# Two tables of a planned decode kernel replaced: the moves of its four engine lists, and the constant products in TensorE's list

## The chip, the cores and the metric

The kernel runs on one core of one Trainium2 chip. The metric is the device time of one execution in microseconds. A measurement of it is the median over several executions; the profile is of one execution more, with a time of its own. The core has TensorE (PE, matmuls), VectorE (DVE), ScalarE (ACT), GpSimd (POOL), SyncE (SP, which issues the loads) and 16 DMA engines that move data from the chip's memory into the core's own memory.

## The reference

One new token for each of four sequences goes through two identical layers: attention over a cache of 4096 keys and values, then a gated feed-forward block, each behind a layer norm without weights and with its input added. Both layers use the same caches and the same weights; everything is bf16.

```python
def attention(x, k_cache, v_cache, wq, wo):      # x: 4 x 1 x 512
    q = heads(x @ wq)                            # 32 query heads of 128, 4 to a K/V head
    k = repeat(k_cache, 4); v = repeat(v_cache, 4)   # caches: 4 x 8 x 4096 x 128
    p = softmax(q @ k.T * 128 ** -0.5)
    return concat_heads(p @ v) @ wo              # wo: 4096 x 512

def feed_forward(x, w_gate, w_up, w_down):       # 512 x 1792, 512 x 1792, 1792 x 512
    return (sigmoid(x @ w_gate) * (x @ w_up)) @ w_down

x = x + attention(layernorm(x), ...)
x = x + feed_forward(layernorm(x), ...)
x = x + attention(layernorm(x), ...)             # the same caches and weights again
x = x + feed_forward(layernorm(x), ...)
```

The bytes are in the caches: 4 x 8 heads x 4096 x 128 x 2 bytes is 33.6 MB for K and as much for V, and the second layer needs them a second time, apart from what the kernel keeps.

## The kernel before

The work is cut into 16 units: one batch row, one half of the K/V heads (four of eight) and one layer each. A string, UNITS, gives their order, in which the rows run staggered: row 0 has finished its first layer while row 2 has not begun. K and V come in pieces of 0.5 MB (half a head, 2048 keys) into a ring of 27 slots, some as a whole head of 1 MB in two slots, and a list names those that are kept for the second layer. All 155 loads are issued by SyncE into one queue, in a written order, and a load waits until the last reader of its slot is done.

A unit runs so. VectorE transposes a K slot in place (line 853). TensorE multiplies it with the row's queries into S_ps (L864), four 512-column matmuls side by side on strips of the array. VectorE takes the maximum (L887), ScalarE the exponentials (L901), TensorE turns them through PT_ps (L912), and with the V slots they give O_ps (L999). Then the output projection wo (L1022, L1044, or L943 and L958 by rows) adds to the row's x.

After the last unit of a row in the first layer comes that row's **chain**, a string of small dependent steps on one row: layer norm (TensorE L1127, L1131 and VectorE L1135), gate and up products (L1201), the sigmoid through a tanh on ScalarE and the product on VectorE (L1244), the down product (L1258), the new x and the sums for the next layer norm (L1104 is the matmul that adds them up), and the queries of the second layer (L759 to L830). The rows' chains stand at about 81 to 98, 123 to 140 and 188 to 205 us for rows 0 to 2 and 232 to 250 us for row 3. A last chain, for all rows that end in the second layer, stands at 270 to 282 us, behind the last load.

The order is not the program's. Every operation is first recorded with its engine, cost, rank and dependences; then `schedule` places all of them in time by a model of the engines and the loads, assigns ring slots, and leaves one list per engine. Then `rearrange` edits these lists by two tables:

- MOVES: each word is one move. `p28>22` takes the operation at place 28 of TensorE's list and inserts it at place 22. The letters are s (SyncE's loads), a (ScalarE), p (TensorE) and d (VectorE), and the words act one after the other.
- FILLS: each word is one **constant product**, a matmul of a constant 128 x 128 matrix with constant columns into a bank that nobody reads before it is written anew (line 1446). `87.2.d64.a17` puts one of 2 x 256 columns ahead of place 87 of TensorE's list (as it is after the moves), and makes it wait for operation 64 of VectorE's list and 17 of ScalarE's. A first wait letter a chooses the bank PT_ps, d the bank G_ps. The result is used for nothing; such a product keeps TensorE at work.

`emit` then writes each engine's list, with a semaphore wait for each dependence that is not yet met on that engine. Ring slots and the tiles of all other operations are chosen before `rearrange` and do not depend on the tables.

Of the kernel before, what the change touches and what calls it, by code (L numbers as in the profile page):

```python
# [32 lines left out]
MOVES = "s21>0 s2>1 s8>2 s4>3 s14>4 s19>5 s13>6 s9>7 s9>8 s18>9 s15>10 s15>11 s19>12 s20>13 s21>14 s21>15 s21>16 s21>17 s20>18 s23>20 s23>21 s24>23 s27>25 s29>27 s30>28 s31>29 s34>33 s40>39 s45>44 s53>52 s58>57 s62>61 s71>70 s78>75 s78>76 s84>83 s87>86 s91>89 s91>90 s94>93 s102>101 s103>102 s118>115 s119>118 s120>119 s123>122 s124>123 s127>126 s136>134 s147>145 s147>146 s150>148 s150>149 s151>150 a2>1 a3>2 a7>6 a12>11 a24>23 a25>24 a31>30 a34>33 a35>34 a42>40 a42>41 a43>42 a44>43 a45>44 a46>45 a59>58 a61>60 a66>65 a67>66 a68>67 a70>68 a74>73 a75>74 a76>75 a77>76 a78>77 a79>78 a80>79 a81>80 a82>81 a83>82 a84>83 a85>84 a87>85 a87>86 a88>87 a89>88 a90>89 a92>90 a92>91 a94>92 a94>93 a96>94 a96>95 a97>96 a98>97 a99>98 a100>99 a101>100 a115>114 a120>119 a121>120 a125>124 a126>125 a127>126 a128>127 a142>141 p3>2 p28>22 p29>24 p28>25 p30>29 p40>39 p41>40 p45>41 p43>42 p44>43 p45>44 p46>45 p50>46 p48>47 p51>48 p50>49 p61>60 p62>61 p63>62 p71>65 p72>67 p93>90 p94>91 p97>92 p131>130 p132>131 p133>132 p134>133 p156>154 p157>156 p158>157 p159>158 p160>159 p161>160 p162>161 p163>162 p165>164 p166>165 p167>166 p168>167 p169>168 p171>169 p172>170 p173>171 p174>172 p175>173 p175>174 p184>183 p215>213 p222>217 p223>218 p224>219 p223>221 p230>226 p236>235 p237>236 p238>237 p239>238 p240>239 p241>240 p244>242 p250>249 p251>250 p252>251 p274>273 p275>274 p276>275 p283>282 p284>283 p285>284 p286>285 p287>286 p288>287 p292>291 p293>292 p294>293 p295>294 p300>297 p302>301 p303>302 p304>303 p305>304 p306>305 p307>306 p308>307 p310>308 p311>309 p312>310 p313>311 p313>312 p314>313 p315>314 p321>320 p322>321 p323>322 p344>342 p344>343 p345>344 p351>349 p352>350 p353>351 p373>371 p377>374 p405>403 p408>407 p410>409 p411>410 p412>411 p413>412 p414>413 p422>420 p423>422 p424>423 p425>424 p431>430 p432>431 p433>432 p434>433 p435>434 p436>435 p437>436 p441>437 p439>438 p440>439 p441>440 p443>442 p448>443 p445>444 p446>445 p447>446 p448>447 p459>455 p463>462 p464>463 p465>464 p466>465 p474>473 p481>479 p482>480 p503>499 p507>503 p508>504 p506>505 p507>506 p509>507 p509>508 p510>509 p533>532 p537>533 p541>538 p542>541 p560>559 p562>560 p593>592 p594>593 p602>600 p604>603 p605>604 p607>606 p633>631 d2>0 d14>1 d18>2 d16>3 d18>4 d18>6 d23>8 d21>10 d21>11 d27>12 d23>13 d15>14 d28>15 d28>17 d28>18 d29>20 d23>21 d27>22 d28>23 d32>24 d26>25 d27>26 d31>27 d41>32 d34>33 d35>34 d36>35 d37>36 d41>39 d43>42 d44>43 d46>44 d47>45 d48>47 d49>48 d51>50 d53>51 d53>52 d57>56 d60>59 d86>80 d82>81 d91>88 d90>89 d93>92 d95>93 d96>95 d97>96 d98>97 d99>98 d101>99 d102>101 d103>102 d105>103 d105>104 d107>105 d107>106 d108>107 d109>108 d120>119 d121>120 d126>124 d126>125 d128>127 d134>133 d136>134 d137>136 d141>139 d142>140 d143>141 d143>142 d144>143 d146>144 d148>145 d149>146 d149>147 d151>148 d152>149 d154>150 d154>151 d155>153 d158>154 d157>155 d159>157 d162>158 d161>159 d163>160 d166>162 d164>163 d165>164 d169>165 d170>166 d172>167 d172>170 d172>171 d174>172 d174>173 d175>174 d177>175 d178>176 d180>178 d180>179 d181>180 d182>181 d183>182 d184>183 d185>184 d186>185 d187>186 d188>187 d192>191 d193>192 d196>194 d202>201 d206>205 d207>206 d208>207 d209>208 d210>209 d211>210 d212>211 d213>212 d215>214 d217>216 d218>217 d219>218 d221>219 d222>220 d225>224 d230>226 d229>228 d232>231 d239>233 d241>235 d237>236 d239>238 d240>239 d247>246 d253>252 d254>253 d262>261 d265>264 d282>281 d283>282 d284>283 d285>284 d286>285 d287>286 d292>291 d295>293 d313>312 d314>313 d315>314 d316>315 d317>316 d318>317 d320>319 d322>321 d324>323 d328>327 d330>329"  # L33
# [55 lines left out]
class _Plan:  # L89
# [61 lines left out]
    def schedule(self):  # L151
# [205 lines left out]
        self.prog = {e: sorted((o for o in self.ops if o.eng == e), key=lambda o: (o.start, o.n)) for e in ENGINES}  # L357
        if FILLS:
            self.rearrange(fillers)
# [10 lines left out]
    def rearrange(self, fillers):  # L370
# [3 lines left out]
        queue["p"][:] = [op for op in queue["p"] if id(op) not in gone]  # L374
        for word in MOVES.split():
            i, j = map(int, word[1:].split(">"))
            queue[word[0]].insert(j, queue[word[0]].pop(i))
        ahead = {}
        for word in FILLS.split():
            at, n, *waits = word.split(".")  # L380
# [1108 lines left out]
```

## Time and profile before

| | |
|---|---|
| three runs | 287.33, 285.98, 284.43 us (median 285.98) |
| the profiled execution | 283.75 us, its span from first to last instruction 281.9 us |
| mean granted TensorE clock in the span | 0.958 |
| busy: TensorE, VectorE, ScalarE | 205.7, 159.0, 67.2 us |
| loaded | 106.70 MB, 378 GB/s over the span |
| constant products | 226, of them 111 of 256 columns |

How to read it: times are of one execution. The page cuts the span into 40 slices; a digit of an engine's row is the busy share in tenths, of the row PEclk the TensorE clock that was granted. A row of a table of stretches gives the stretch, its length, busy time and count for PE, PEld (weight loads), DVE, ACT and POOL, the granted clock, the DMA share and GB/s. A timeline row gives start, duration, engine, line, operation, what is written from what, how many instructions, and in brackets the idle time before and what ended it. A matmul's row includes the time in which it runs through the array, so that rows overlap.

### The profile page before, as it was taken

How to read it: one execution, taken by the hardware profiler on the slowest of the kernel's cores; microseconds unless marked ns; L12 is line 12 of the kernel's file. 1: busy time of each engine (PE TensorE's matmuls, PEld its weight loads, DVE VectorE, ACT ScalarE, POOL GpSimd, SP SyncE). 2: the span in 40 equal slices, each digit the busy share in tenths (PEclk: the TensorE clock that was granted, in tenths of full speed). 3: DMA queues.
4: the chain of work that ended last, by engine and by line, in shares of the span. 5: the costliest groups of instructions: out<-in, count | busy, mean ns of one | idle time of the engine just before them, and what ended most of it. 6: DMA issues, size and time to landing. Idle time of an engine off the chain costs nothing.

```text
span 281.9 us, 7386 instructions
## 1 busy us (share of the span) xinstructions
PE 205.7 (73%) x3212; PEld 102.0 (36%) x3212; DVE 159.0 (56%) x347; ACT 67.2 (24%) x169; POOL 15.7 (6%) x61
## 2 busy tenths in 40 slices
PE   0000068729779899998998768889886889899975
PEld 0000022303246542465533212346532346555453
DVE  1479924143502278713398799438469827976333
ACT  1000021200422231342311400431324142235411
POOL 8300010000000000000000000000000000000011
PEclk9999999957995899999999979999999999999999
DMA  7999999999999799999999999999999999999920
GB/s 282 420 422 414 410 388 389 381 428 412 401 402 408 262 353 421 418 414 404 398 392 413 417 420 424 427 406 411 409 408 406 417 416 400 352 381 391 409 80 3
DMA packets 27536, 107.18 MB, mean 380 GB/s; under 512 B 2544, under 2 KB 6640, under 8 KB 23408
## 3 DMA queue, kind: packets, MB, share of 16 engines
q1 hardware_dynamic: 27440, 106.70, 95.4%
q8 instruction: 25, 0.41, 0.6%
q14 instruction: 7, 0.06, 0.1%
q10 hardware_dynamic: 64, 0.01, 0.0%
HBM read 106.70 MB, written 0.00 MB: 378 GB/s over the span
## 4 chain that ended last, share of the span: by engine, by line
DMA 42%; PE 34%; DVE 13%; ACT 4%; issue 3%; SPq 3%; POOL 1%; DVEq 0%
DMA ring<-in_A_k_cache_dram 22%; DMA ring<-in_A_v_cache_dram 16%; DVE ring L853 9%; PE S_ps L864 7%; PE O_ps L999 5%; DMA wo<-in_A_wo_dram 4%; PE PT_ps L1446 3%; PE G_ps L1258 3%; SPq L607 2%; PE G_ps L1446 2%; PE G_ps L1201 1%; PE M_ps L1044 1%; ACT b L1014 1%; PE Q_ps L958 1%; DVE qz L830 1%
## 5 line engine op out<-in xcount | busy, mean ns | idle before, releaser
L853 DVE STREAM_TRANSPOSE ring<-ring 128x1024 int32<-128x1024 int32 x86 | 103.1, 1223 | 27.1 <-DMA ring<-in_A_k_cache_dram 26.6
L999 PE MATMUL O_ps<-ring,pt_sb 128*16 128x512 bf16 x472 | 38.4, 394 | 8.7 <-DMA ring<-in_A_v_cache_dram 5.4
L864 PE MATMUL S_ps<-ring,qz 128*32 128x512 bf16 x512 | 40.5, 415 | 3.8 <-DVE qz L830 2.1
L1446 PE MATMUL PT_ps<-even 128*128 128x512 bf16 (+1 forms) x114 | 35.7, 346 | 7.0 <-DVE ring L853 3.5
L1446 PE MATMUL G_ps<-even 128*128 128x512 bf16 (+1 forms) x112 | 34.3, 347 | 2.8 <-DVE qz L830 1.2
L1014 ACT ACTIVATE b<-O_ps 128x512 bf16<-128x512 f32 x32 | 19.1, 596 | 62.0 <-PE O_ps L999 53.0
L864 PEld LDWEIGHTS S_ps<-ring,qz 128*32 128x32 bf16 x512 | 12.3, 98 | 20.3 <-issue 5.1
L1446 PEld LDWEIGHTS PT_ps<-even 128*128 128x128 bf16 x114 | 11.0, 103 | 23.8 <-issue 10.7
L887 DVE TENSOR_REDUCE stat<-S_ps 128x1 f32<-128x512 f32 x16 | 10.9, 679 | 12.4 <-PE S_ps L864 12.2
L901 ACT ACTIVATE pp<-S_ps,tr 128x512 bf16<-128x512 f32 x16 | 13.4, 836 | 18.7 <-DVE tr L894 13.9
L999 PEld LDWEIGHTS O_ps<-ring,pt_sb 128*16 128x16 bf16 x472 | 9.0, 87 | 22.2 <-issue 9.8
L830 DVE TENSOR_TENSOR qz<-Q_ps,maskrs 128x256 bf16<-128x256 f32 x16 | 6.4, 400 | 17.8 <-PE Q_ps L820 16.1
L1446 PEld LDWEIGHTS G_ps<-even 128*128 128x128 bf16 x112 | 10.6, 106 | 15.6 <-issue 8.7
L825 ACT ACTIVATE maskrs<-mask,stat 128x16 f32<-128x16 f32 x16 | 4.8, 302 | 44.8 <-POOL stat L709 36.2
L922 ACT ACTIVATE pt_sb<-PT_ps 128x512 bf16<-128x512 f32 x16 | 9.6, 597 | 16.1 <-PE PT_ps L912 16.0
L677 PE MATMUL M_ps<-even,b 16*128 16x16 bf16 x1 | 0.2, 191 | 17.8 <-DVE M_ps L579 17.8
L1174 POOL TENSOR_TENSOR stat<-stat 128x1 f32<-128x1 f32 x5 | 2.7, 540 | 179.3 <-DVE stat L1170 179.3
L907 DVE STREAM_TRANSPOSE pp<-pp 128x256 int32<-128x256 int32 x16 | 6.9, 434 | 6.9 <-ACT pp L901 6.9
L1022 PE MATMUL M_ps<-sel_o,b 128*128 128x32 bf16 x108 | 7.0, 178 | 5.2 <-DVE oT L1028 3.0
L1022 PEld LDWEIGHTS M_ps<-sel_o,b 128*128 128x128 bf16 x108 | 4.9, 96 | 13.4 <-ACT b L1014 7.2
L689 PE MATMUL U_ps<-stat 128*128 128x4 f32 x2 | 0.6, 366 | 12.2 <-DVE stat L685 12.2
L1044 PE MATMUL M_ps<-oT,wo 128*128 128x32 bf16 x256 | 8.5, 178 | 1.1 <-DVE oT L1028 0.6
(157 smaller groups left out, 239.0 us busy)
## 6 DMA issues: line engine op xcount, KB each, us to landing
ring<-in_A_v_cache_dram SPq DMA_DIRECT2D x61, 512.0 KB, 9.6
ring<-in_A_k_cache_dram SPq DMA_DIRECT2D x54, 512.0 KB, 7.9
ring<-in_A_k_cache_dram SPq DMA_DIRECT2D x16, 1024.0 KB, 8.6
ring<-in_A_v_cache_dram SPq DMA_DIRECT2D x15, 1024.0 KB, 9.3
wq<-in_A_wq_dram SPq DMA_DIRECT2D x2, 2048.0 KB, 18.8
wo<-in_A_wo_dram SPq DMA_DIRECT2D x4, 1024.0 KB, 18.0
wg<-in_B_w_gate_dram SPq DMA_DIRECT2D x1, 1792.0 KB, 18.9
wu<-in_B_w_up_dram SPq DMA_DIRECT2D x1, 1792.0 KB, 15.3
```

The source lines that it names most:

```text
L830: lambda e: e.tensor_tensor(qz[qi][:, 16:].rearrange("p (n x) -> p n x", x=32)[:, :, 0:16].rearrange("p n (a h) -> p n a h", h=R), Q_ps[:, ...
L853: "dve", lambda e, t=t: e.transpose(ring[t.slot].bitcast(dt.int32), ring[t.slot].bitcast(dt.int32)),
L864: fns.append(lambda e, s=s, t=t, nn=nn, q=q: e.matmul(S_ps[qi][32 * s:32 * s + 32, :], lhsT=window(qi, s * NQ + nn, q), rhs=ring[t.slot].r ...
L887: dve(lambda e: e.tensor_reduce(ml[at], bank, AX.X, ALU.max, negate=True), keys(f"S{qi}", ss), keys("ml", ss), 0.6)
L901: lambda e: e.activation(p_sb[at].rearrange("p (t j r) -> p t r j", j=32, r=2), bank.rearrange("p (t r j) -> p t r j", r=2, j=32), ACTF.Ex ...
L922: "act", lambda e: e.activation(pt_sb[qi][:, cols], PT_ps[:, cols], ACTF.Copy),
L999: fns.append(lambda e, m=m, at=at, v=ts[s2], c=c, q=q, final=final: e.matmul(O_ps[m:m + 16, :], lhsT=pt[:, at:at + 16], rhs=ring[v.slot][: ...
L1014: "act", lambda e: e.activation(b1[:], O_ps[:], ACTF.Copy),
L1022: fns.append(lambda e, tt=tt: e.matmul(M_ps[:, 0:WIDE], lhsT=b1[:, tt * P:(tt + 1) * P], rhs=sel_o[:, tt, :].unsqueeze(1).broadcast_to([P, ...
L1044: fns.append(lambda e, k=k, n=n, h0=h0, split=straight: e.matmul(M_ps[:, k * WIDE:(k + 1) * WIDE], lhsT=wo[:, h0 + n, k * P:(k + 1) * P], ...
L1258: fns.append(lambda e, k=k, c=c, rows=rows: e.matmul(o_ps[:, k * WIDE:(k + 1) * WIDE], lhsT=wd[:, c, k * P:(k + 1) * P], rhs=rows.unsqueez ...
L1446: return lambda n: lambda e: e.matmul(bank[:, 0:256 * n], lhsT=ident, rhs=flat_even[:, 0:256 * n], start=True, stop=True)
```

## The change

Two strings are replaced, lines 33 and 34; every other line is the same. MOVES has 488 words instead of 432 (s 58 for 54, a 90 for 57, p 175 for 160, d 165 for 161). FILLS has 82 words instead of 226: 41 products into PT_ps for 114, 41 into G_ps for 112, and 30 of 256 columns for 111. In the built lists the first product of the new kernel stands ahead of L1127 of the first chain (row 0), the second between that L1127 and L1131; the next comes in the unit after the chain. All loads are the same pieces into the same slots; where the two orders differ is mostly among the first 25 loads.

```diff
-MOVES = "s21>0 s2>1 s8>2 s4>3 s14>4 s19>5 s13>6 s9>7 s9>8 s18>9 s15>10 s15>11
...
-a2>1 a3>2 a7>6 a12>11 a24>23 a25>24
...
-p3>2 p28>22 p29>24 p28>25 p30>29 p40>39 p41>40 p45>41
...
-d2>0 d14>1 d18>2 d16>3 d18>4 d18>6 d23>8 d21>10
...
-FILLS = "18.1.d9.d33 18.2.d9.d37 24.1.d9.d33 24.2.d9 26.2.d9.d38 27.1.d9 33.2.a8.a9 35.1.d9 36.1.d9.d39 39.1.a8.d42 39.2.d9 39.2.d9.d39 39.2.a8 39.1.a8 39.2.d9.d43 39.1.d9.d40 39.1.a8 42.2.a8.d41 46.1.a8.d46 50.2.d9.d46 52.2.d9 52.2.a8.a12 53.2.a8 53.2.a8.d51 54.2.d9.a13 54.2.d9 55.2.d9.d55 56.2.a15.d52 58.1.a15.d53 60.2.d9 60.2.d9 72.2.d9
-87.1.d64.d64 87.1.a18 101.2.a18 103.1.a18.d73 142.1.d77
...
-599.2.d277 599.1.a135 599.1.d277 599.1.a135.d298 606.1.a135 624.2.d314 634.1.a135.d320 634.1.a135"
+MOVES = "s8>0 s4>1 s4>2 s13>3 s6>4 s18>5 s10>6 s16>7 s12>8 s19>9 s21>10 s21>11
...
+a3>1 a4>2 a5>4 a7>5 a8>6 a9>8
...
+p3>2 p28>18 p29>20 p30>22 p31>25 p32>31 p33>32 p34>33
...
+d19>0 d28>1 d23>2 d21>4 d7>5 d23>6 d22>7 d32>8
...
+FILLS = "87.2.d64.a17 88.2.d64.d66 152.1.a37 158.2.a37 168.1.d77.d97 179.2.d77 185.2.d77 198.2.a45.d110 199.2.a45.d112 201.1.a45.a46 203.2.a45.a45 212.2.d115 212.2.d115.d116 230.2.a45 258.2.a45.a56 259.1.d130.a59 267.2.d130.d136 267.2.d130 268.2.d130 268.2.a45 280.1.a45 300.2.a69 323.2.d130.d176 323.2.d130.a72 324.2.d130 324.1.a69.d178 325.2.d130 325.2.d130.d175
...
+498.2.d253 499.1.d253.d259 499.2.a107 506.2.a107 527.2.a107 542.1.d277 542.2.d277 557.2.a121 558.2.a121 558.2.d277.d286 559.1.d277 559.1.a121 559.2.a121.a127 559.1.d277.d288 599.2.a135 599.2.a135.a135 599.2.a135 606.2.a135.a136 623.2.a135.d316 649.1.d332"
```

The strings are one line each in the file; they are broken here by engine.

4 lines of the change are left out of this document (2 added, 2 removed).

## The prediction

> **What bounds the kernel now.** I read the page first: the slices, the queues, the chain that ended last and the groups of the constant products (line 1446).
>
> ```profile
> span 281.9 us, 7386 instructions
> ...
> PEclk9999999957995899999999979999999999999999
> DMA  7999999999999799999999999999999999999920
> GB/s 282 420 422 414 410 388 389 381 428 412 401 402 408 262 353 421 418 414 404 398 392 413 417 420 424 427 406 411 409 408 406 417 416 400 352 381 391 409 80 3
> ...
> q1 hardware_dynamic: 27440, 106.70, 95.4%
> q8 instruction: 25, 0.41, 0.6%
> ...
> DMA 42%; PE 34%; DVE 13%; ACT 4%; issue 3%; SPq 3%; POOL 1%; DVEq 0%
> ...
> L1446 PE MATMUL PT_ps<-even 128*128 128x512 bf16 (+1 forms) x114 | 35.7, 346 | 7.0 <-DVE ring L853 3.5
> L1446 PE MATMUL G_ps<-even 128*128 128x512 bf16 (+1 forms) x112 | 34.3, 347 | 2.8 <-DVE qz L830 1.2
> ```
>
> 106.7 MB go through one queue, and the DMA row is 9 nearly everywhere until the last two slices. So the stream of loads bounds the kernel, and after it stands a tail. The 226 products take 70.0 us of TensorE's time, but an engine that feeds a full queue loses nothing by it. So the second view is a table of stretches that I cut at the dips of the GB/s row, with DMA share and GB/s as the last columns:
>
> ```profile
> 84.00:92.00 8.00, 7.31 (x136) 4.99 (x137) 2.34 (x13) 2.03 (x6) 0.54 (x1) 0.50 0.99 407
> 92.00:104.00 12.00, 10.49 (x200) 6.04 (x196) 5.48 (x15) 3.83 (x13) 0.54 (x1) 0.91 0.82 290
> 104.00:140.00 36.00, 33.67 (x589) 17.72 (x589) 18.29 (x48) 11.23 (x30) 1.08 (x2) 1.00 1.02 413
> 140.00:147.00 7.00, 6.64 (x63) 2.20 (x58) 5.89 (x6) 0.84 (x2) 0.00 (x0) 1.00 1.01 393
> 147.00:180.00 33.00, 26.39 (x274) 9.26 (x275) 27.03 (x41) 5.77 (x13) 0.00 (x0) 0.95 1.02 416
> ...
> 237.00:256.00 19.00, 16.64 (x349) 10.20 (x353) 16.63 (x38) 6.37 (x21) 1.08 (x2) 1.00 0.99 365
> ...
> 269.00:282.00 13.00, 8.55 (x223) 6.35 (x223) 4.57 (x29) 2.30 (x7) 1.90 (x3) 1.00 0.04 14
> ```
>
> With 413 GB/s as the full rate, 92–104 loses 12.0 × (1 − 290/413) = 3.6 us, 237–256 loses 19.0 × (1 − 365/413) = 2.2 us and 140–147 loses 0.3 us. These 6.1 us and the tail of 13 us are all that an order of work can win back; the rest is bytes. Everything else the change does is judged by whether it delays a load.
>
> Who stops the loads? One row of SyncE's waits (sum, times, longest), its issue after the large hole in the timeline, and what the loads issued in three short stretches took from issue to landing (last column, us):
>
> ```profile
> SPq L607 <- PE U_ps L1104: 20.0, 2, 16.2
> ```
>
> ```profile
> 94.52 0.81 SPq L607 DMA_DIRECT2D ring<-in_A_k_cache_dram  x2
> ```
>
> ```profile
> ring<-in_A_k_cache_dram SPq DMA_DIRECT2D x2, 512.0 KB, 3.9
> ring<-in_A_k_cache_dram SPq DMA_DIRECT2D x4, 512.0 KB, 5.1
> ring<-in_A_k_cache_dram SPq DMA_DIRECT2D x2, 1024.0 KB, 8.0
> ```
>
> The last three are for issues in 94–95, 141–144 and 157–163. From 78.3 to 94.52 SyncE stood 16.2 us at a ring slot that L1104, the last matmul of the first feed-forward chain (row 0), sets free; behind it stood every later load. At 94.52 nothing was queued, and the first two loads took 3.9 us, so about 3.3 us is one load into an empty queue (3.9 less half of a transfer of 0.524 MB / 0.413 = 1.27 us). What is above that is cover, the time by which an issue may be late: an estimate of 5.1 − 3.3 = 1.8 us at 141–144, 8.0 − 3.3 − 1.3 = 3.4 us at 157–163 (a load of twice the size).
>
> **The change part by part.** It reorders four engines' lists and takes 144 of 226 constant products out. I count a product of 512 columns as one unit, a half one as half, and four 512-column matmuls side by side also as one. The edits remove about 104 of 170 units. What a unit costs, and what a cold clock costs, stands in these rows (TensorE's timeline; then L1201 in two stretches and L1258 in two, where the third column from the right is the granted clock):
>
> ```profile
> 40.97 1.47 PE L864 MATMUL S_ps<-ring,qz 128*32 128x512 bf16 x12 [0.58 <-DVE qz L830]
> ...
> 81.33 0.60 PE L943 MATMUL Q_ps<-wo,oT 128*1 128x512 bf16 x8 [0.74 <-DMA wo<-in_A_wo_dram]
> ...
> 142.38 0.82 PE L1446 MATMUL PT_ps<-even 128*128 128x256 bf16 x4
> ...
> 243.49 1.08 PE L864 MATMUL S_ps<-ring,qz 128*32 128x512 bf16 x16 [0.53 <-DVE ring L853]
> ```
>
> ```profile
> 88.20:91.40 3.20, 3.13 (x48) 1.53 (x48) 0.50 1.02 410
> 240.90:242.80 1.90, 1.78 (x48) 1.04 (x48) 1.00 1.04 397
> ```
>
> ```profile
> 91.70:93.80 2.10, 1.91 (x56) 1.80 (x56) 0.50 0.76 297
> 244.40:246.20 1.80, 1.57 (x56) 1.47 (x56) 1.00 1.05 373
> ```
>
> A full-clock unit is (1.08 − 0.17)/4 = 0.23 us, a half-clock one (1.47 − 0.17)/3 = 0.43 us, where 0.17 is the overlap I take off a row for its last matmul. So a unit pays 0.2 us more when cold; the weight-bound L1258 only 1.91 − 1.57 = 0.34 us in 56; L1201 1.35 us in 48.
>
> In this execution the granted clock changes in steps of 3.41 us (cold from 56.6 to 66.9, 83.9 to 94.2, 165.9 to 169.3). Counting units per step from the timeline, steps with 6 or more were followed by full clock, steps with 5 or fewer by half clock, and one with 5.9 that began cold left it cold. Step 80.5–83.9, with L943's two units and one product, held 3 and made the first chain cold, although the kernel before had its products. With the old times and the new products, the steps newly below 6 are those of 70–77 (1, 5 units), 101–111 (3, 5, 4.5), 145–149 (4), 152–172 (1, 5, 5, 1, 3, 3, of which the fourth was low before) and 210–217 (2, 3.5). Around the chains of rows 1 to 3 and at the end the products stay.
>
> The Trainium skill, "TensorE: Matmul & The Clock Gate", section "HAM oscillation — how this bites in real kernels", speaks against the change: idle gaps of more than about 3.4 us drop the clock to half, and the next work starts cold. The trace agrees on the step of 3.41 us; it differs in that a step with some work, 3 units, is enough to drop it. Were the rule only about whole idle steps, no product here would matter for the clock, and only the gains below would stand.
>
> Step by step, as a difference to the profiled execution:
> - To 84 us: every product goes and the early loads are permuted; TensorE starts 0.5 to 1 us later at most, since one load more stands ahead of wq. The bytes ahead of the second half of wo are the same, and L943 waits for it at 81.3, so the chain starts when it did: 0. This cover goes if the landing of wo moves.
> - First chain, 84–94.5: a product and a half around L1258 go (1.5 × 0.43 = 0.65), two half ones ahead of L1127 become a whole one, and one product comes between L1127 and L1131 (+0.3, cold). With it, step 87.3–90.8 counts 6.9 units instead of 5.9; if that makes it warm from 90.8, L1258's 0.34 and some 0.4 of the matmuls after it go too. Range −1.1 to +0.3, taken −0.6. Every microsecond here is a microsecond of the stream, as the queue is empty at 94.5.
> - 101–118: the three steps from 104.4 run cold, 16 units at +0.2 = 3.2 us, against 13.5 units of products gone from them (3.1 us at full clock): 0, with ends −0.5 and +1.7 (for lack of cover, below).
> - 140–147: four half products stood between two score groups (0.82 us) and more around them, ahead of which loads waited; the dip of 0.3 us goes: −0.3, from −0.5 to 0.
> - 147–180: 29 units fall into newly cold steps, 5.8 us, against 17.5 units of products gone from them (4.0 us); single releases come 0.5 to 1 us later, under 3.4 of cover: 0, ends −0.2 and +1.7.
> - 210–221: 9 units in two newly cold steps, +1.8, less 5.5 units of products gone (1.3 us): +0.5 under a cover of 1.8 at the least: 0.
> - 237–256: K landing, its transpose on VectorE (16.6 us busy of 19) and score, then slot again, are a closed loop in both orders: 0, ends −1.1 (half its loss) and +0.5.
> - Tail: the two half products inside L1201 go, one unit: −0.2.
>
> Sum −1.1, so 282.65 for the profiled execution of 283.75 us (span 281.9 and 1.85 around it). That one is the fastest of four known executions (287.33, 285.98, 284.43, 283.75; mean 285.37), and nothing in it says what the others paid. I set the sum against the mean: 285.37 − 1.1 = 284.3.
>
> **Rivals.**
> *Slower: the cold clock delays loads.* Place: ring slots freed by scores and values in 101–118 and 147–180. If the gone products lay in waits anyway, the half clock is a net cost: 3.2 us against 1.8 of cover makes 1.4, 5.8 against 3.4 makes 2.4, together 3.8 or 285.4 + 3.8 = 289.2; if the last chain falls cold as well (264.8–268.3 holds just 6 units), L1201 and L1258 add 1.7: 290.9. I take 289.2. It decides from the point at which a release is later than its cover. For it: PE was busy 33.67 of 36 us in 104–140, and the step after 101 clearly falls below 6. Against: about as many units of products go as the half clock adds.
>
> *Faster: the first chain is warm and the hole closes.* If the clock is back from 87.3, L1201 gives 1.35, L1258 0.34, products 0.65, together 2.3 us of the 3.6 that the hole loses; with 0.3 at 140, 0.2 in the tail and half of 237–256's 2.2 it is −3.9: 281.5. For it: the chain of waits gives 34% to PE, and products stand in it. Against: step 83.9–87.3 counts 5.
>
> *TensorE's program transfers.* A late one would stop TensorE; 288 instructions fewer (144 products with their weight loads) are about one transfer of 25. If the slower executions held such stops and the new order does not, the time is the profiled one's less 0.6: 283.1. Against: in the timeline each idle gap of TensorE over 0.25 us has an operand that came late, so not one stop is seen. The Trainium skill, "Runtime: NRT & Kernel Launch", section "Instruction fetch mechanics", has the engine fetch the next block of 256 instructions while it runs the present one; by that rule this rival is nothing, and q8's 25 transfers agree in number.
>
> *Nothing:* the stream is full either way: 285.4. I count it with the forecast.
>
> **How the numbers follow.** Forecast, with nothing, 0.50; first chain warm 0.24; cold delays 0.21; transfers 0.05. A 1% change, 2.86 us, is about what a measurement here can tell from none: faster is below 283.1, slower above 288.8. Faster: 0.24, half of transfers and some 0.04 of the forecast's low end: 0.30. Slower: 0.17 of the cold case and 0.04 of the forecast, since four executions spread over 3.6 us: 0.21. Same: 0.49. The forecast's own range is 282.8 to 286.5; the range takes in most of the warm case and half of the cold one: 281.0 to 289.0.
>
> **What would show it.** Right: granted clock 0.5 in 104–114 and in much of 148–176 with GB/s still above 405 there; the wait at L1104 ending within 1 us of 94.5; 140–147 at 410; 237–256 near 365; a tail of 12 to 13 us. Wrong: a new dip of GB/s behind a cold stretch, a hole at 92–104 that is gone or longer, or idle time of TensorE that no operand explains.

## The result, and the profile after

| | before | changed |
|---|---|---|
| median of 20 executions each | 284.49 us (281.85 to 287.33) | 285.33 us (284.0 to 288.01) |
| ratio changed / before, 95% interval | | 1.0062 [1.0037, 1.0086] |
| the profiled execution | 283.75 us, span 281.9 us | 285.46 us, span 283.7 us |
| mean granted TensorE clock | 0.958 | 0.880 |

The changed kernel is slower by about 0.6%, little but more than the interval: the sign of the forecast's −1.1 us was wrong. Measured once more (12 executions), the ratio was 1.0045 [1.0020, 1.0071]. Over all sessions, 149 executions of the kernel before have a median of 284.00 us and 33 of the changed one 285.39 us: +1.4 us. (The ratios leave out executions more than 1.5% above a kernel's fastest, so that one can lie beside the ratio of its medians.)

The page of the changed kernel, the lines that answer to those of the kernel before:

```profile
span 283.7 us, 7098 instructions
...
PEclk9999999966567995999967556999995899999999
DMA  6999999999999799999999999999999999899920
GB/s 252 418 422 421 411 411 364 387 419 416 401 405 407 257 394 424 410 412 411 359 384 426 419 419 418 422 410 409 409 385 411 412 419 388 341 356 377 412 91 3
...
q8 instruction: 24, 0.39, 0.5%
...
L1446 PE MATMUL G_ps<-even 128*128 128x512 bf16 (+1 forms) x41 | 14.1, 365 | 3.9 <-DVE ring L853 3.6
...
L1446 PE MATMUL PT_ps<-even 128*128 128x512 bf16 (+1 forms) x41 | 14.7, 371 | 0.7 <-ACT b L1014 0.4
```

The products' 70.0 us are now 28.8 us, the clock row has new low digits (counted from 1, slices 11, 12, 16, 21 to 25 and 31), and the GB/s row is nearly the old one, with a deeper dip at slice 20 (359 for 398). The table of stretches, cut as before, and the row of SyncE's wait at the first chain:

```profile
84.00:92.00 8.00, 6.06 (x130) 4.65 (x130) 2.11 (x13) 2.50 (x8) 0.54 (x1) 0.79 1.00 411
92.00:104.00 12.00, 9.07 (x192) 5.45 (x192) 4.95 (x15) 4.31 (x15) 0.54 (x1) 1.00 0.83 308
104.00:140.00 36.00, 31.55 (x560) 15.91 (x564) 17.78 (x49) 11.54 (x29) 1.08 (x2) 0.91 1.02 409
140.00:147.00 7.00, 3.61 (x40) 0.87 (x28) 6.22 (x6) 0.00 (x0) 0.00 (x0) 0.79 1.00 359
147.00:180.00 33.00, 22.75 (x252) 8.28 (x250) 28.34 (x44) 7.04 (x16) 0.00 (x0) 0.63 1.02 421
...
207.00:217.00 10.00, 6.64 (x96) 3.30 (x95) 7.73 (x17) 3.59 (x10) 0.00 (x0) 0.76 0.98 395
...
237.00:256.00 19.00, 17.25 (x339) 10.16 (x340) 16.81 (x38) 5.79 (x19) 1.08 (x2) 1.00 0.90 350
```

```profile
SPq L607 <- PE U_ps L1104: 19.5, 2, 15.5
```

Read against the prediction's rows, one pair of profiles tells three things. Where TensorE ran longest at half clock (147–180, mean 0.63), the loads came at 421 GB/s for 416: the cold clock there cost no load. The hole at 92–104 looks better, 308 for 290, as forecast. 140–147 is worse, 359 for 393, where a gain was forecast. But a pair of profiles is weak evidence for 0.6%, so both kernels were profiled three times in all.

### The profile page after: what moved, and what is told of

It reads as the page before. It is cut to its first block, busy times and chain, and to the rows that moved or that the text cites. A ratio compares the mean times of both kernels' runs of the same rounds, so it can differ in the third digit from the quotient of the medians.

```text
span 283.7 us, 7098 instructions
## 1 busy us (share of the span) xinstructions
PE 188.7 (67%) x3068; PEld 94.9 (33%) x3068; DVE 159.2 (56%) x347; ACT 66.6 (23%) x169; POOL 15.8 (6%) x61
## 4 chain that ended last, share of the span: by engine, by line
DMA 37%; PE 34%; DVE 16%; ACT 5%; issue 4%; SPq 2%; POOL 0%; DVEq 0%; ACTq 0%
DMA ring<-in_A_v_cache_dram 18%; DMA ring<-in_A_k_cache_dram 18%; DVE ring L853 11%; PE S_ps L864 9%; PE O_ps L999 7%; PE G_ps L1258 2%; SPq L607 2%; ACT b L1014 1%; PE G_ps L1446 1%; PE Q_ps L943 1%; ACT pp L901 1%; PE PT_ps L912 1%; PE Q_ps L797 1%; PE Q_ps L718 1%; PE M_ps L1044 1%
## 5 line engine op out<-in xcount | busy, mean ns | idle before, releaser
L999 PE MATMUL O_ps<-ring,pt_sb 128*16 128x512 bf16 x472 | 43.2, 448 | 17.0 <-issue 6.4
L864 PE MATMUL S_ps<-ring,qz 128*32 128x512 bf16 x512 | 44.0, 458 | 9.5 <-DVE ring L853 4.6
L864 PEld LDWEIGHTS S_ps<-ring,qz 128*32 128x32 bf16 x512 | 13.6, 107 | 31.2 <-DVE ring L853 10.3
L999 PEld LDWEIGHTS O_ps<-ring,pt_sb 128*16 128x16 bf16 x472 | 9.8, 91 | 30.7 <-issue 16.6
L1446 PE MATMUL G_ps<-even 128*128 128x512 bf16 (+1 forms) x41 | 14.1, 365 | 3.9 <-DVE ring L853 3.6
L1446 PE MATMUL PT_ps<-even 128*128 128x512 bf16 (+1 forms) x41 | 14.7, 371 | 0.7 <-ACT b L1014 0.4
L926 PE MATMUL M_ps<-sel_h,stat 128*128 128x16 f32 x32 | 7.5, 311 | 5.4 <-ACT pp L901 5.4
L912 PE MATMUL PT_ps<-pp,even 128*32 128x128 bf16 x256 | 8.0, 259 | 2.6 <-DVE oT L1028 1.3
L727 ACT ACTIVATE pp<-Q_ps 128x512 bf16<-128x512 f32 x2 | 1.2, 592 | 35.9 <-PE Q_ps L718 35.9
L926 PEld LDWEIGHTS M_ps<-sel_h,stat 128*128 128x128 f32 x32 | 6.4, 241 | 9.3 <-ACT pp L901 7.3
L1028 DVE TENSOR_TENSOR oT<-M_ps,rl 128x8 bf16<-128x8 f32 x27 | 4.1, 151 | 9.1 <-PE M_ps L1022 9.1
```

Of the source, the lines that this page charges most:

```text
L864: fns.append(lambda e, s=s, t=t, nn=nn, q=q: e.matmul(S_ps[qi][32 * s:32 * s + 32, :], lhsT=window(qi, s * NQ + nn, q), rhs=ring[t.slot].r ...
L912: fns.append(lambda e, s=s, a=a: e.matmul(PT_ps[32 * a:32 * a + 32, s * P:(s + 1) * P], lhsT=ident[at, 32 * s:32 * s + 32], rhs=spread[:, ...
L926: "pe", lambda e: e.matmul(M_ps[:, hs], lhsT=ls[at].broadcast_to([len(ss) * 32, P]), rhs=sel_h[at, hs], start=True, stop=True,),
L999: fns.append(lambda e, m=m, at=at, v=ts[s2], c=c, q=q, final=final: e.matmul(O_ps[m:m + 16, :], lhsT=pt[:, at:at + 16], rhs=ring[v.slot][: ...
L1446: return lambda n: lambda e: e.matmul(bank[:, 0:256 * n], lhsT=ident, rhs=flat_even[:, 0:256 * n], start=True, stop=True)
```

## The experiments

The theories at the start were these. *Loads:* a changed order of loads opened the dip at 140–147. *Products:* the missing products, by the clock or by what they held back, cost the time. *Transfers:* the transfers of TensorE's program fall at other places and hold something. *First chain:* the gain forecast there is not there. (The expectations name them by letters: L is loads, C products and the clock, H transfers, K a warm first chain, F a gain that is lost again further on, S the start of the stream, E the end.)

### Three profiles of each

Both kernels unchanged, each profiled again beside the other experiments: the changed kernel first,

> The new kernel unchanged, for a second profile of it and as the reference for the other three. Ratio 1.004 to 1.009. Theory C (cold clock by the phase of the 3.41 us steps): in another execution the steps fall elsewhere on the work, so other stretches are cold and the dips of GB/s lie elsewhere. Theory L (load order): the dip in 139-147 is there again, with 340 to 370 GB/s, whatever the phase.

> The new kernel unchanged, a third profile. Theory S and the first chain: 4 MB at 12.4 to 12.6 us, L958 of the first chain from 83.1 on, 114 us for 44 MB give or take 0.3; what comes behind is chance.

and the kernel before.

> The kernel before unchanged, for a second profile and its own scatter: ratio 0.998 to 1.002. Theory H: the execution's time goes with the issues that a transfer meets. Theory C: with its mean granted clock.

> The kernel before unchanged, a third profile. 4 MB at 12.0 to 12.3 us, L958 of the first chain at 82.4 to 82.7, 44 MB at 113.4 to 114.2 us.

Measured: changed 285.44 us (283.05 to 286.84; the ratio is given above), third time 283.32 us in one execution; before 283.85 us, ratio to itself 0.9986 [0.9951, 1.0021], third time 282.03 us. GB/s by stretch, from the tables of the six profiles:

| profile | its time | 92–104 | 104–140 | 140–147 | 147–180 | 207–217 | 237–256 |
|---|---|---|---|---|---|---|---|
| before, 1 | 283.75 | 290 | 413 | 393 | 416 | 410 | 365 |
| before, 2 | 283.91 | 309 | 411 | 393 | 417 | 415 | 339 |
| before, 3 | 282.03 | 310 | 411 | 407 | 418 | 413 | 361 |
| changed, 1 | 285.46 | 308 | 409 | 359 | 421 | 395 | 350 |
| changed, 2 | 283.05 | 302 | 413 | 373 | 421 | 392 | 375 |
| changed, 3 | 283.32 | 309 | 413 | 378 | 421 | 388 | 362 |

The rows behind the two steadiest columns, of the third profile of the changed kernel and then of the kernel before:

```profile
140.00:147.00 7.00, 3.71 (x32) 0.67 (x24) 6.52 (x6) 0.00 (x0) 0.00 (x0) 0.72 0.97 378
...
207.00:217.00 10.00, 5.86 (x90) 3.17 (x94) 7.73 (x18) 4.01 (x10) 0.00 (x0) 0.72 1.00 388
```

```profile
140.00:147.00 7.00, 6.57 (x63) 2.31 (x52) 6.75 (x7) 0.78 (x2) 0.00 (x0) 1.00 1.02 407
...
207.00:217.00 10.00, 6.67 (x93) 3.07 (x86) 8.65 (x19) 4.31 (x11) 0.00 (x0) 1.00 1.02 413
```

What follows: the profile of before that the prediction was read from had the worst first chain of three (290 GB/s; the others 309 and 310), so the changed kernel's 302 to 309 is no gain. 237–256 is scatter in both (339 to 375). Two stretches are worse in all three, 140–147 and 207–217.

To see what lasts, I summed the bytes of the queue by the time at which they had landed, and took the mean of three profiles against the mean of three:

| MB landed | 34 | 44 | 60 | 82 | 86 | 95 | last load | time |
|---|---|---|---|---|---|---|---|---|
| about at, us | 87 | 114 | 153 | 207 | 216 | 238 | 272 | |
| changed later by, us | 0.17 | 0.24 | 0.36 | 0.35 | 0.88 | 0.82 | 0.72 | 0.71 |

One step is clear of the scatter, that in 207–216: from 82 to 86 MB the three profiles of the kernel before take 9.79, 9.70 and 9.74 us, those of the changed kernel 10.20, 10.25 and 10.37, which is 0.53 us more on the mean. The others lie within the scatter between executions: 0.17 us up to 34 MB (0.32 if it is read at 33 MB), 0.07 from there to 44 MB, the first chain, and 0.12 from 44 to 60 MB, where the dip at 140–147 costs 7 × (397.7 − 370)/413 = 0.47 us, of which 147–180 gives most back. Together this is 0.7 of the 1.4 us between the medians; single executions of one kernel spread over 4 to 5 us, and the rest is not placed.

### Parts of the change undone

The one move of the load list that exchanges the K loads ahead of the dip at 140–147, taken out:

```diff
 MOVES
...
-s70>69
...
```

> The new kernel with three neighbours of SyncE's list put back in the old order (two K pieces of row 2's first unit that wait for line 999's values of row 1, and one of row 1's second layer). Theory L (load order): in the new order a piece whose slot is free at 134.7 stands behind one whose slot comes free at 136.9, nothing is issued for 2.2 us, and the stream falls to 359 GB/s in 140-147; with the old order that stretch is back at 390 GB/s or more and the kernel is about 1.0 us faster than the new one: ratio to before 1.002 to 1.003 (new: 1.006). Theory C (cold clock): nothing to do with these loads, ratio stays 1.005 to 1.007.

Measured 286.49 us, ratio 1.0030 [0.9977, 1.0084]. Its 140–147 has 396 GB/s, but its 147–180 only 405 for 421: the dip moved. Whether the time followed is not told: the ratio is what the loads theory expected (1.002 to 1.003), the median is no lower than that of the changed kernel, and the interval takes in both theories.

Of the old products, 110 put back into the changed order in the stretches that had turned cold (70–84, 100–118, 144–178 and 209–222 us); and, the other way round, the old order with 98 of its 226 products:

```diff
 FILLS of the changed kernel, 192 words for 82
+51.2.d5 52.2.d5 52.2.a6 53.2.d5.a12 53.2.d5 54.2.a14.a6
...
 FILLS of the kernel before, 98 words for 226
-18.1.d9.d33 18.2.d9.d37 24.1.d9.d33 24.2.d9 26.2.d9.d38
...
```

> The new kernel with 110 of the old kernel's constant products put back ahead of the same matmuls in 70-84, 100-118, 144-178 and 209-222 us, the stretches that the new tables leave cold. Theory C: the granted clock is 1.0 there again (mean from 0.88 to about 0.95) and the time falls to that of the kernel before, ratio 0.998 to 1.001. Theory L: the clock comes back, but the loads had cover in these stretches (421 GB/s in 147-180 at clock 0.63), so ratio 1.004 to 1.008.

> The kernel before with its own order and 98 of its 226 products: those before 86, in 90-118, 147-178 and 208.5-222 us are left out, as the new tables have it. Theory C: it is slower by the same 0.6% as the new kernel, ratio 1.004 to 1.008, with GB/s lower behind the cold stretches. Theory L: products cost and give nothing here, ratio 0.998 to 1.002, though the mean clock is near 0.88.

Both are slower than either kernel, and by more than any theory expected: products back 288.45 us, ratio 1.0159 [1.0110, 1.0209]; old order with fewer products 289.95 us, ratio 1.0207 [1.0154, 1.0260]. First the former's stretches, then the latter's:

```profile
92.00:104.00 12.00, 9.77 (x210) 5.65 (x204) 4.64 (x16) 4.22 (x15) 0.54 (x1) 0.94 0.77 285
...
130.00:147.00 17.00, 13.47 (x243) 7.21 (x245) 8.83 (x20) 4.03 (x15) 1.08 (x2) 0.90 0.95 360
```

```profile
92.00:104.00 12.00, 9.40 (x206) 5.58 (x198) 5.63 (x17) 4.12 (x13) 0.54 (x1) 0.91 0.74 272
...
180.00:208.00 28.00, 24.36 (x450) 13.48 (x446) 15.57 (x43) 8.13 (x21) 0.54 (x1) 0.95 0.99 386
```

In medians that is a square: old order with its products 284.0, with 98 of them 289.95; new order with its 82 products 285.4, with 192 it is 288.45. Fewer products cost the old order some 6 us, and more products cost the new order some 3 us. So each order goes with its own products, and the new moves make up for most of what missing products cost the old order. The clock alone can't be the measure, since the new order with more products runs at a mean clock of 0.92 to 0.94 and is slower than with few at 0.88.

Then the tables of the changed kernel up to some 97 us with the old ones behind, and up to some 233 us with the old ones behind:

```diff
 first: MOVES and FILLS of the changed kernel, the old words from these places on
+s45>44 s58>57 s78>75 a35>34 p156>154 d86>80
...
 second: likewise
+s136>134 a125>124 p482>480 d254>253
...
```

> The new tables up to about 97 us (43 loads, 126 TensorE operations with their 2 products), the old tables behind that. By the two traces the new first part takes 0.75 us out of the hole at 92-104 and has lost 0.5 us in the first 5 us of the stream. If the 0.5 us is chance of one execution: ratio 0.996 to 0.998. If it belongs to the new order of the first loads: 0.998 to 1.000. Theory C: the first chain is no colder than before, so it says the same; it would be wrong with a ratio above 1.002.

> The new tables up to about 233 us, the old ones behind that. The traces of the two kernels differ by 1.1 us of stream between 238 and 258. If the end's own order or products make that (theory E): ratio 1.001 to 1.004. If the end only repeats what came late into it, the K pieces, their transposes, scores and the slots they free following one another (theory F): the 1.1 us are lost again and the ratio is 1.005 to 1.009.

Measured 286.72 us, ratio 1.0109 [1.0057, 1.0160], and 285.76 us, ratio 1.0032 [0.9993, 1.0071]. The new first part before the old rest reads worse than the whole change, though the intervals overlap. It doesn't place the loss in that part: in its profile the stream is 0.20 us behind the mean of the kernel before at 34 MB, 1.54 at 44 MB and 3.41 at 60 MB, so most is lost at the join and behind it. With the old end the ratio is 0.1 to 0.3% below that of the whole change, which is not told from nothing.

Last, the load list alone: the changed kernel with the old list of SyncE, and the kernel before with the new one.

```diff
 changed kernel, 54 words for 58
-s8>0 s4>1 s4>2 s13>3
+s21>0 s2>1 s8>2 s4>3
...
 kernel before, 58 words for 54
-s21>0 s2>1 s8>2 s4>3
+s8>0 s4>1 s4>2 s13>3
...
```

> The new kernel with the whole of SyncE's list as before; the other three lists and the 82 products are the new ones. Theory L: the 0.4 us lost in the first 5 us of the stream and the 0.7 us of 139-150 go, ratio 1.001 to 1.004. Theory C: the loads are not the point, ratio 1.004 to 1.010; and an order of loads that the other lists were not made for may itself cost, which would put it above 1.010.

> The kernel before with the new SyncE list only. Theory L: it takes over the loss of the new loads, 0.4 + 0.7 us: ratio 1.003 to 1.005, with the stream at 340 to 370 GB/s in 139-147. Theory C: ratio 0.998 to 1.002 at a mean clock of 0.95 to 0.96.

These were the largest effects of all, and no theory expected them: 296.66 us, ratio 1.0436 [1.0395, 1.0477], and 301.22 us, ratio 1.0584 [1.0548, 1.0621]. More than half of it is one hole. The stretch 56–67 us of the former, of the latter, and of the kernel before:

```profile
56.00:67.00 11.00, 7.19 (x98) 3.14 (x94) 3.72 (x9) 3.17 (x8) 0.00 (x0) 0.82 0.42 143
```

```profile
56.00:67.00 11.00, 9.03 (x98) 3.08 (x95) 3.04 (x7) 1.89 (x5) 0.00 (x0) 0.84 0.15 51
```

```profile
56.00:67.00 11.00, 5.70 (x35) 1.59 (x33) 6.03 (x6) 0.91 (x2) 0.00 (x0) 0.53 1.02 423
```

The early loads are late for what the engines have been told to do first, so slots come free late, and the stream stands: one load waits 12.7 us in the former and 17.2 us in the latter for a slot that L864 sets free. No list of the change can be judged by itself: each half of it alone costs more than the whole.

### The transfers of TensorE's program

The 24 transfers of 16 KB (q8) begin at nearly the same places of TensorE's list in all three profiles of a kernel, on the mean 255 to 259 matmuls and weight loads apart in the changed one, so products of 16 columns ahead of everything shift them: 64 and 8 of them (128 and 16 instructions) in the changed kernel, 80 (160 instructions) in the kernel before.

```diff
-        return lambda n: lambda e: e.matmul(bank[:, 0:256 * n], lhsT=ident, rhs=flat_even[:, 0:256 * n], start=True, stop=True)
+        return lambda n: lambda e: e.matmul(bank[:, 0:256 * n or 16], lhsT=ident, rhs=flat_even[:, 0:256 * n or 16], start=True, stop=True)
...
+1.0.d5 1.0.d5 1.0.d5 1.0.d5
...
```

> The new kernel with 64 constant products of 16 columns more in TensorE's list, ahead of its second and third operation, where it idles between 22 and 37 us. They do no work; they move every later transfer of TensorE's program by 128 instructions, half a block. Theory H (hold): a load issue that meets a program transfer takes 1.0 to 1.5 us instead of 0.33 to 0.44, and in the new kernel the transfers at 131.4, 137.3 and 251.3 meet issues that the stream waits for; moved by half a block they meet fewer (by my count of its trace 1 instead of 3 with little cover): 0.5 to 1.5 us faster than the new kernel, ratio 0.999 to 1.003, and issues over 0.9 us long are at other places. Theory C (clock, order): nothing changes, ratio 1.003 to 1.007.

> The same with 8 such products, a move of 16 instructions or about 0.4 us. Theory H: by the count the transfers then meet the issues at 131, 137.0, 140.7 and 250.8, the worst place of all: ratio 1.006 to 1.011. Theory C: 1.003 to 1.007.

> The kernel before with 80 such products, a move of 160 instructions. In its own trace no transfer meets an issue with little cover behind 95 us; moved so, by the count, they meet those at 135.5, 200.6, 206.0 and 245.6. Theory H: it gets slower by 1 to 2 us, ratio 1.003 to 1.008. Theory C: ratio 0.998 to 1.002.

Measured 285.88 us, ratio 1.0033 [0.9995, 1.0070]; 284.90 us, 1.0031 [0.9995, 1.0066]; 283.77 us, 1.0013 [0.9978, 1.0048]. No shift moved a median by more than 0.2% from that of its own kernel, and the two that were expected to cost 0.3% and more by the transfers did not show it. So nothing here makes the transfers the cause; an effect of some tenths of a per cent is within the intervals. They do hold single loads, which is told at the end.

### A warm first chain

If the half clock over the first chain sets the hole at 92–104, products ahead of it should close the hole. Sixteen whole products around 60 to 80 us in the changed kernel; then fifteen, with the group of L999 that waits for its V piece put behind the L1044 groups; and eight in the kernel before:

```diff
 changed kernel
+53.2.d5 53.2.d5 53.2.d5 58.2.d5 58.2.d5 60.2.d5 60.2.d5 61.2.d5 61.2.d5 61.2.d5 72.2.d5 73.2.d5 73.2.d5 74.2.d5 74.2.d5 74.2.d5
...
 the second has in MOVES besides
-p71>61
+p62>61
...
-p66>65
+p71>65
...
 kernel before
+70.2.d9 70.2.d9 70.2.d9 73.2.d9 73.2.d9 74.2.d9 74.2.d9 74.2.d9
```

> The new kernel with 16 constant products of 512 columns more, ahead of TensorE operations that wait for something between 72 and 86 us, so that each step of 3.41 us there holds 6 units and the first chain runs at full clock. Theory K (the first chain's clock): no half clock between 73 and 95, SyncE's issue behind L1104 comes 0.5 to 1.5 us before 94.4, the hole at 92-104 shrinks by as much, ratio 0.998 to 1.002 instead of 1.005, with less scatter. Theory F (the gain is lost again): the hole shrinks, but the stream is back at the old place by 150, and the ratio stays 1.003 to 1.006.

> The same, and the first values matmul group of row 0's second value half, which waits for its V piece until 79.1, stands behind the four L1044 groups instead of ahead of them, as in the old order. In the new order these begin at 79.65 instead of 77.92, and L958 of the first chain at 83.35 instead of 82.42. Theory K: the chain ends another 0.5 to 0.9 us earlier, ratio 0.995 to 0.999. Theory F: 1.002 to 1.006.

> The kernel before with 8 constant products more where TensorE waits between 80.6 and 84.9 us. Theory K: no half clock between 77 and 95, L1104 1.5 to 2.3 us earlier (L1201 takes 1.78 instead of 3.13 us, L1258 1.57 instead of 1.91), ratio 0.993 to 0.997. Theory F: 0.998 to 1.003, with the stream ahead by 1 us or more at 105 and level again by 150.

Measured 286.25 us, ratio 1.0037 [0.9998, 1.0076]; 285.81 us, 1.0057 [1.0022, 1.0093]; 284.02 us, 0.9997 [0.9969, 1.0026]. First the changed kernel with sixteen, then the kernel before with eight:

```profile
84.00:92.00 8.00, 6.02 (x133) 4.23 (x133) 1.92 (x12) 2.17 (x8) 0.54 (x1) 1.00 1.00 411
92.00:104.00 12.00, 9.62 (x190) 5.49 (x190) 4.11 (x15) 3.95 (x14) 0.54 (x1) 0.86 0.77 281
```

```profile
84.00:92.00 8.00, 6.23 (x145) 4.60 (x147) 2.54 (x14) 2.03 (x6) 0.54 (x1) 1.00 1.01 414
92.00:104.00 12.00, 9.79 (x196) 5.87 (x199) 5.23 (x15) 3.83 (x13) 0.54 (x1) 1.00 0.84 328
...
130.00:147.00 17.00, 15.57 (x259) 7.81 (x254) 8.58 (x18) 3.56 (x13) 0.54 (x1) 0.93 0.98 367
```

Both have the full clock over 84–92. In the changed kernel the wait at L1104 still ends at 94.3 us and the hole stays. In the kernel before, the hole has 328 GB/s for 290 to 310 in the three plain profiles; L1104 begins at 93.78 us for 94.20 on their mean, and the stream is 0.5 us ahead of that mean at 44 MB. By 57 MB it is 1.0 us behind (367 GB/s over 130–147), and the median didn't move. Two rows of the latter show why the chain gained so little:

```profile
89.54 0.46 PE L1201 MATMUL O_ps<-wu,small 128*1 128x192 bf16 x12
...
91.61 0.36 PE L1258 MATMUL G_ps<-pp,wd 128*128 128x32 bf16 x8 [1.60 <-DVE b L1235]
```

L1201 runs from 88.22 to 90.00 us instead of 88.27 to 91.43, as the prediction priced it, but L1258 begins at 91.61 instead of 91.76: it then waits 1.60 us for VectorE. So the rival was right about the clock and wrong about the path. At full clock the middle of the chain waits for the steps on ScalarE and VectorE, L1104 comes 0.4 us earlier and not 2.3, and even that was lost at the next place where loads wait for slots.

The first two loads exchanged, so that the half-sized one is first, was a try at an earlier start:

```diff
-s8>0 s4>1
+s3>0 s8>1
...
```

> The new kernel with its first two loads exchanged, so that the first is 0.5 MB, as in the old order, and not 1 MB. Theory S (start): 4 MB have landed 0.2 to 0.35 us earlier than in the new kernel (12.5 us), the second half of wo lands and the first chain's L958 begins as much earlier, and the kernel gains 0.1%: ratio 1.002 to 1.006, which the times alone can't tell from the new kernel's 1.0045. If the start is chance: 12.5 us again.

Measured 285.37 us, ratio 1.0067 [1.0025, 1.0109]: the first 4 MB landed at 12.04 us, for 12.24 to 12.53 in the changed kernel, and nothing of it reached the end.

## Why the prediction was wrong, point by point

**The bound held.** Loads bound both kernels, and each term was rightly put as a delay of loads. The profiles show no stop of TensorE over 0.5 us without an operand that came late: where the page of the changed kernel puts 6.4 us ahead of L999 down to "issue", a V piece landed 0.09 us before each of the three groups began.

**"To 84 us … 0" failed by 0.2 to 0.3 us in the stream and 0.5 us at the chain's start.** TensorE's timeline of the changed kernel ahead of the first chain (start, duration, line, operation, idle time before it):

```profile
77.82 0.29 PE L1022 MATMUL M_ps<-sel_o,b 128*128 128x32 bf16 x4 [0.71 <-ACT b L1014]
79.11 0.60 PE L999 MATMUL O_ps<-ring,pt_sb 128*16 128x512 bf16 x4 [1.00 <-DMA ring<-in_A_v_cache_dram]
79.65 1.03 PE L1044 MATMUL M_ps<-oT,wo 128*128 128x32 bf16 x32
80.61 0.62 PE L912 MATMUL PT_ps<-pp,even 128*32 128x128 bf16 x16
81.01 1.84 PE L943 MATMUL Q_ps<-wo,oT 128*1 128x512 bf16 x16
82.69 0.39 PE L999 MATMUL O_ps<-ring,pt_sb 128*16 128x512 bf16 x4
83.35 0.61 PE L958 MATMUL Q_ps<-stat,b 128*128 128x1 f32 x4 [0.28 <-ACT b L953]
```

The prediction had named the condition, "this cover goes if the landing of wo moves", and it did move. In all six profiles the second half of L943 begins 0.04 to 0.05 us behind the landing of the second half of wo, at 81.96, 81.78 and 81.35 us in the changed kernel for 81.29, 81.52 and 81.39: on the mean 0.30 us later. The first 4 MB of the stream were late by as much (12.53, 12.49 and 12.24 us for 12.06, 12.22 and 12.12), and the run with the half-sized load first had 12.04 and 81.47. Behind L943 a group of L999 stands where the kernel before has a constant product, and the clock is at half up to 82.6, 82.2 and 81.7 us: from L943's second half to L958 it takes 1.24 to 1.35 us for 1.09. So L1127, the chain's first matmul, began at 88.15, 87.92 and 87.44 us for 87.29, 87.43 and 87.36, 0.48 us later on the mean.

The wait of 1.00 us that the rows show, of a moved group of L999 for its V piece ahead of the 32 matmuls of L1044, looks like the cause and isn't. In the run that put this group behind L1044:

```profile
78.12 0.96 PE L1044 MATMUL M_ps<-oT,wo 128*128 128x32 bf16 x32 [0.26 <-DVE oT L1028]
...
82.13 0.60 PE L943 MATMUL Q_ps<-wo,oT 128*1 128x512 bf16 x8 [1.72 <-DMA wo<-in_A_wo_dram]
...
83.22 0.62 PE L958 MATMUL Q_ps<-stat,b 128*128 128x1 f32 x4
```

L1044 starts as early as in the kernel before, TensorE then waits 1.72 us for wo, and L958 is no earlier.

**"First chain … taken −0.6" was right in the chain and nothing in the sum.** From L1127 to L1104 the changed kernel takes 6.11, 6.15 and 6.21 us, for 7.11, 6.78 and 6.62: on the mean 0.68 us shorter, with the product between L1127 and L1131 in it. The late start takes 0.48 of it, and L1104 begins at 94.26, 94.07 and 93.65 us, for 94.40, 94.21 and 93.98. Of the 0.20 us that are left the stream shows nothing: from 34 to 44 MB it takes 27.12, 27.39 and 27.17 us for 27.54, 27.02 and 26.89. This is the larger of the two steps that failed: 0.6 us was taken off the stream for the chain's length, and its start was put at 0. Besides, the chain was priced from the coldest of three executions.

**"140–147 … −0.3" had the wrong sign.** The half products that stood between the score groups are gone, and the dip is deeper (359, 373, 378 GB/s for 393, 393, 407), and TensorE's time was not the limit there: it was busy for 3.61 of the 7 us, for 6.64 before. The loads were issued late. Part of this may be the transfers of TensorE's program: in all three profiles of the changed kernel an issue at 137.1 to 137.6 us met one and took 1.30 to 1.48 us, in those of the kernel before none did there. In the run shifted by 128 instructions no issue there is long and the stretch has 404 GB/s; but the run with the first two loads exchanged has 366 with none over 0.8 us between 133 and 144 us, so this stays open.

**"210–221 … under a cover of 1.8 at the least: 0" is the other step that failed, with the largest loss.** The loss is 0.5 us, in 207–217. It isn't the half clock that was priced: in the one-microsecond slices of the changed kernel the loads thin out at 209–211 us, ahead of the cold stretch. Two slices of the kernel before stand below them:

```profile
208.00:209.00 1.00, 1.00 (x17) 0.37 (x16) 0.12 (x1) 0.00 (x0) 0.00 (x0) 1.00 1.01 406
209.00:210.00 1.00, 1.00 (x19) 0.34 (x16) 0.08 (x1) 0.00 (x0) 0.00 (x0) 1.00 0.79 303
210.00:211.00 1.00, 0.30 (x9) 0.19 (x5) 0.93 (x3) 0.60 (x1) 0.00 (x0) 1.00 0.93 352
...
213.00:214.00 1.00, 0.50 (x16) 0.23 (x12) 1.00 (x2) 0.44 (x1) 0.00 (x0) 0.50 0.98 397
```

```profile
209.00:210.00 1.00, 0.46 (x10) 0.00 (x0) 0.69 (x1) 0.50 (x2) 0.00 (x0) 1.00 1.09 422
210.00:211.00 1.00, 0.65 (x8) 0.33 (x9) 0.92 (x5) 0.54 (x4) 0.00 (x0) 1.00 0.95 397
```

Two further runs say the same. The first row is the kernel with one move of the loads taken out, the second the one with the first two loads exchanged:

```profile
207.00:217.00 10.00, 6.15 (x96) 2.55 (x97) 6.11 (x14) 3.38 (x9) 0.00 (x0) 0.93 0.95 380
```

```profile
207.00:217.00 10.00, 6.36 (x96) 3.12 (x94) 7.59 (x17) 3.42 (x9) 0.00 (x0) 0.79 1.02 413
```

The one with the clock at 0.93 loses more, the one with the clock at 0.79 nothing.

What failed is the measure of cover. The prediction took 3.3 us for a load into an empty queue, of which 1.27 us is its transfer, so an issue was to be early enough with 2.0 us of work left in the queue. I worked this out for each load behind 30 us in 18 profiles (all but the two third ones): the time left is from its issue to the landing of all bytes issued before it, the loss is its own landing time beyond its bytes at 413 GB/s:

| left at issue, us | loads | mean loss, us |
|---|---|---|
| under 1 | 20 | 1.85 |
| 1 to 1.5 | 32 | 0.49 |
| 1.5 to 2 | 41 | 0.15 |
| 2 to 2.5 | 108 | 0.24 |
| 2.5 to 3 | 116 | 0.17 |
| 3 to 3.5 | 168 | 0.10 |
| 3.5 to 4 | 212 | 0.05 |
| 4 to 7 | 816 | 0.01 |

So losses begin under some 3.5 us, not under 2.0: the cover was overstated by more than 1 us. The two loads behind the waits at L864 and L797 at 205 to 208 us are issued with 2.4 to 3.04 us left in all six plain profiles. They lost 0.59, 0.73 and 0.74 us in the changed kernel's and 0.12, 0.09 and 0.12 in the kernel before's. Over the nine profiles that have the changed order and its products there the loss is 0.07 to 1.72 us, 0.65 on the mean; over the five with the old, 0.07 to 0.46, 0.17 on the mean. That place in the table is one where an issue sometimes loses. The loss seems to go with the order, not with the products: with 110 products put back into the new order the same two loads lost 1.03 us, at full clock, and with 98 products in the old order 0.06, in one profile each. What in the new order makes it stays open: the time left is nearly the same, and the clock, by the two rows above, does not tell.

**"101–118" and "147–180" at 0 were right,** and with them the odds against the rival of a cold clock that delays loads: long half-clock stretches in new places, 409 to 413 GB/s over 104–140, 421 over 147–180. The Trainium skill, "TensorE: Matmul & The Clock Gate", section "HAM oscillation — how this bites in real kernels", prices a drop of the clock as matmul time doubled; the trace agrees for TensorE (0.43 us for 0.23 us a unit), and shows that in these two stretches none of this time was on the path of the loads. The prediction took the 0.43 from a row at 40.97 us, where the page of the kernel before has the clock at 9; a row of the changed kernel inside its half-clock stretch, (1.90 − 0.17)/4, gives the same:

```profile
171.18 1.90 PE L864 MATMUL S_ps<-ring,qz 128*32 128x512 bf16 x16 [3.32 <-DVE ring L853]
```

**237–256** was right too, 362 GB/s on the mean for 355. **The tail** was put at −0.2 and did not change: 11.9 us from the last landing to the end of the time in both kernels.

**The level.** The number 284.3 lay near the result only because the four executions that it was set against had a mean of 285.37; the median of 149 is 284.00. As a difference the forecast was −1.1 us and the result +0.7 (means of three profiles) to +1.4 us (medians). By its terms, with the ledger's stretches for the measured ones: before the chain 0 became +0.17, the first chain −0.6 became +0.07, 140–147 −0.3 became +0.12 with what follows it, 207–217 0 became +0.53, the rest and the tail −0.2 became −0.18. Only +0.53 is clear of the scatter; the forecast gain of the first chain and of 140–147 is what is missing beside it.

**The rivals.** Slower came neither by the cold clock nor by one large wait, but by a few tenths at two places. The warm first chain was tried: it was worth 0.4 us and not 2.3, and that was lost later. The program transfers moved no median clear of noise. "Nothing" was the nearest.

## What to carry to other kernels

Price a stage from several profiles, and set the start of a chain beside its length: the chain was priced from the coldest of three executions, and its start was held by a load. Before pricing a faster engine, look who would be waited for next: at full clock this chain waited for VectorE. A queue that looks full still has places where the next load is issued just in time; rank the issues by the work left in the queue, and take those under about 3.5 us (in this kernel) as places at which an edit loses or gains. Lists that were sought together (loads, moves, fill-in work) are judged together: the load list alone, exchanged either way, cost 4 to 6%, the whole change 0.5%.

## What the runs showed of the hardware that was not expected

**A program transfer holds SyncE, not TensorE.** In the changed kernel's profile, SyncE's two issues at the dip of 140–147, and the queue of the program in that microsecond:

```profile
137.32 1.95 SPq L607 DMA_DIRECT2D ring<-in_A_k_cache_dram  x2
```

```profile
q8 instruction: 1, 0.02, 6.8%
```

The first of the two issues took 1.48 us; the transfer began at 137.34 us. In all 20 profiles, behind 85 us, 2288 load issues have a median of 0.43 us, and 97 took over 0.85 us; for 69 of the 97 a transfer of TensorE's program began during the issue or at most 0.3 us before. Of 159 issues that met one, those 69 were long (0.9 to 1.6 us). The Trainium skill, "Runtime: NRT & Kernel Launch", section "Instruction fetch mechanics", says that the cost of crossing a block is mostly hidden; the trace agrees for TensorE itself, where the one idle gap at a transfer that the profile's page leaves to "issue" (0.80 us, up to 182.45) ended 0.09 us behind the landing of a V piece. Of the engine that issues loads beside it the section says nothing; here its issues were long. That the transfer is the cause rests on this coincidence in time: 71% of the long issues met one, and 7% of all.

**The clock's steps fall at another phase in each execution.** Stretches of half clock are whole steps of 3.41 us, but the first chain's began at 83.9, 85.8 and 84.1 us in the three profiles of the kernel before and ended at 94.2, 92.6 and 91.0; the first of these is the one with 290 GB/s. Over 129 executions of that kernel, time and mean clock go together with a correlation of −0.47: the third with the lowest clock has a median of 284.81 us, the third with the highest 283.44. That is as much as the whole effect of the change.

**The prediction's count of units per step holds in every profile.** I counted, as the prediction did, the units of TensorE (512 columns at full width, or four matmuls side by side) in each step of 3.41 us from 50 to 262 us, in all 20 profiles. Of 238 steps with under 4.75 units, 234 were followed by half clock; of 798 with 6.75 or more, none; of the 226 between, 72. The long cold stretches of the changed kernel (106.4–113.3, 144.0–150.8 and 154.2–174.7 us) lie close to where the prediction had put them by this count.
